# Attention, layer norm and MLP on one core: the first half of a hand-written instruction order replaced, with six more products of zeros

## The chip, the core and the metric

The kernel runs on one core of one Trainium2 chip, as one launch. The metric is the device time of that launch in microseconds (us). TensorE (PE) does matrix products and transposes into PSUM banks, VectorE (DVE) and ScalarE (ACT) read PSUM and write SBUF, GpSimd (POOL) works on SBUF alone, and SyncE (SP) issues DMA transfers. Each engine takes its instructions in the order of its own list and waits on semaphores for what the others produce. GpSimd issues transfers too, on another DMA queue (q0) than SyncE's (q1).

## The reference

Eight batches of eight heads, sequence 576, head width 64. Attention is causal, with a gate from a running sum; layer norm over the 512 joined columns follows, then an MLP of 512 to 2048 to 512 with a residual.

```python
s_pos = np.maximum(s, 0.0)
cum = np.cumsum(s_pos, axis=-1)
bias = -(cum[:, :, :, None] - cum[:, :, None, :])
scores = np.where(causal, -1000000000.0, scale * q @ k.T + np.minimum(bias, 0.0))
attn = np.exp(scores - scores.max(-1, keepdims=True))
attn = attn / (attn.sum(-1, keepdims=True) + 1e-09)
x = (attn @ v).transpose(0, 2, 1, 3).reshape(B, S, H * D)

xn = (x - mu) / np.sqrt(var + 1e-06) * g_ln
out = x + np.maximum(xn @ w_ch1, 0.0) @ w_ch2      # w_ch1 [512, 2048], w_ch2 [2048, 512]
```

## The kernel before

The whole kernel stands under a manual schedule: each engine's list is in the order in which the program issues the instructions, and that order is written by hand as a string of 1,238 words, `PLAN` (L1288). A loop behind it (L1371) splits every word into a step's name and its arguments and calls the step. A suffix (`:A`, `:D`, `:P`) names the engine that does it. A prefix `n*` sets `ahead[0] = n`: the next PSUM tile that is opened (`ptile`, L91) first gets n products of zeros (L101), which the step's own products overwrite. They have the width of the tile, 512 columns at most.

Batch 0 is done by rows of 128 (tiles 0 to 3, and a last one of 64 rows, 4), in two groups of four heads. For tile t and group g:

- `T.t.g` transposes the k and q rows (L958), `e.t.g` copies them out of PSUM (L156 on DVE, L154 on ACT);
- `S.t.g.i` is one bank of scores (L980, mask by L988), `x.t.g.i` its exponential on ACT (L997); `Sk` and `xk` are the last tile's remaining scores and their exponential (L1009, L1016);
- `V.t.g` weighs v (L1038), `N.t.g` divides by the sums on DVE (L1052, L1063);
- `L.t` is the layer norm (L724 on DVE), `X.t` its transposes (L757), `y.t` the copy out, `M`, `r` the first MLP product in pieces and its relu (L1082, L1093, L1095).

Batch 1 goes head by head: `Q`, `E` (transposes L336, copies L156 or L154), `s`, `d` (scores, L404, L412, L440, L448; their exponentials L415 come with them), `v` and `n` (L597, L609, L611), `ga` (statistics of the layer norm), `l` and `la` (L701, L724), `D` and `Da` (transposes of normed rows by DMA, L746).

Batches 2 to 7 go by pairs of heads. `lr` and `lv` load k, q and v rows on SyncE's queue (L219) into eight staging buffers; `cr` casts rows on GpSimd (L231); `tr` transposes by DMA on SyncE's queue (L238); `vm` and `vo` weigh v by the gate on GpSimd (L246, L258, L259); for batch 2 the transposes are on TensorE instead (`O2`, `F`, `G`, `lp`: L374, L154). `tk` copies the keys of the last tile (L158). `B2.n` is the burst of scores of pair n (L562), `bx` its exponentials on ACT (L567), `bm` the causal masks on GpSimd (L506), `Y.n.i` the weighing of v (L641), `K.n.i` the division on DVE (L658, L659, L661). `sd`, `se`, `sm` are the last tile's scores, exponential and mask of a batch.

Between these stand the units `u` and `U`, taken one by one from a queue that `qu`, `La` and `qm` fill. A unit is four products of 512 columns, either of the first MLP matrix (`ph`, L775), closed by a relu into `hT`, or of the second (`py`, L794), every fourth closed by the residual on DVE (`yo`, L806) and a store. With `u` the relu runs on ACT (L766), with `U` on DVE (L764).

`w2.i` loads a quarter of the second MLP matrix and `lp.n` the k and q rows of a pair of batch 2, both on GpSimd's queue. `aug` and `a3` write the gate's extra rows of the score operands by DMA on SyncE's queue (L278, L280); `a3` overwrites what `Sk` reads and so waits for it.

PSUM is shared out as m 2, s 3, t 2, o 1 banks for batches 0 and 1, and as m 2, s 6 after the word `to` (`to_pairs`, L1110). A tile waits until the last reader of the bank's former tile is done.

Of the kernel before, what the change touches and what calls it, by code (L numbers as in the profile page):

```python
# [30 lines left out]
def fast_path(  # L31
# [1256 lines left out]
    PLAN = """  # L1288
        relur.1 lr.3.0 relu.0 scan.0 scan.1 cq hi.0 qu.1 hi.1 sub.0 mid.0 lo.0 relur.2 sub.1 scan.2 W.4
        tc.0 bc.0 ck.0 6*T.0.1 T.0.0 mid.1 lo.1 tc.1 e.0.1:D bc.1 5*T.1.1 hi.2 sub.2 e.0.0:A S.0.0.0  # L1290
        T.1.0 W.1 m mid.2 lo.2 La.3 tc.2 e.1.1:D x.0.0.0 V.0.0 bc.2 e.1.0:A S.0.1.0 N.0.0 x.0.1.0
        S.1.1.0 x.1.1.0 T.2.1 bc.4 e.2.1:D S.1.1.1 x.1.1.1 T.2.0 S.1.0.1 x.1.0.1 e.2.0:D V.0.1 S.1.0.0
        N.0.1 S.2.1.2 x.2.1.2 T.3.0 x.1.0.0 e.3.0:D qu.2 S.2.0.2 S.2.1.0 x.2.0.2 aug L.0 x.2.1.0 T.3.1
        S.3.0.1 x.3.0.1 V.1.0 e.3.1:D qu.3 La.2 N.1.0 V.1.1 N.1.1 L.1 S.2.0.0 x.2.0.0 S.2.0.1 x.2.0.1
        S.3.0.2 x.3.0.2 X.0 y.0:A S.3.1.2 S.2.1.1 x.2.1.1 V.2.0 N.2.0 x.3.1.2 X.1 y.1:D S.3.0.0 x.3.0.0
        V.2.1 M.0.1.0 B.0.1 M.0.1.3 S.3.0.3 x.3.0.3 M.0.1.2 N.2.1 L.2 M.0.1.1 r.0.1:A M.0.0.0 M.0.0.2
        Q.q.4 B.1.1 O E.q.4.0:A M.0.0.3 E.q.4.1:A V.3.0 N.3.0 S.3.1.1 x.3.1.1 M.0.0.1 r.0.0:D S.3.1.3
        S.3.1.0 T.4.0 e.4.0:D X.2 y.2:D x.3.1.3 Q.k.4 E.k.4.0:D T.4.1 e.4.1:D x.3.1.0 S.4.0.1 x.4.0.1
        S.4.0.0 M.0.2.0 M.0.2.2 x.4.0.0 M.0.2.3 V.3.1 E.k.4.1:D N.3.1 B.2.1 S.4.1.1 x.4.1.1 u d.8 L.3
        M.0.2.1 Q.q.5 r.0.2:D B.1.0 s.8 u X.3 S.4.1.0 x.4.1.0 y.3:D Sk xk E.q.5.1:D E.q.5.0:A B.0.0  # L1300
        B.3.0 a3 u v.8 qu.4 qu.5 Q.k.5 lp.9 E.k.5.0:D u E.k.5.1:D V.4.0 N.4.0 s.9 cr.3.0.1 n.8 V.4.1
        N.4.1 Q.q.6 E.q.6.0:A u B.2.0 d.10 s.10 wr Q.k.6 E.k.6.0:D A.0 v.9 lp.10 w2.2 lr.3.1 E.k.6.1:D
        n.9 u U E.q.6.1:A s.11 Q.k.7 Q.q.7 E.q.7.0:A lp.11 La.6 E.k.7.0:D E.q.7.1:A U U E.k.7.1:D v.10
        n.10 cr.3.0.0 U d.12 s.12 U v.11 n.11 ga.1.0.0 A.2 d.14 s.13 O2.k.9:A u w2.3 B.3.1 v.12 n.12
        ga.1.0.3 s.14 O2.k.8:A A.1 me wT lv.2.0 wx vo.2:P U v.13 n.13 ga.1.1.2 s.15 cr.3.1.1 U O2.q.9:A
        ga.1.0.2 F.k.8 v.14 ga.1.0.1 F.k.9 G.k.9:A n.14 U u A.3 R vm.2.0:P lr.3.2 v.15 cr.3.2.0
        O2.k.11:A lv.2.1 lv.2.2 vm.2.1:P G.k.8:A ga.1.1.1 u lv.2.3 u O2.q.8:A ga.1.1.3 F.q.9 G.q.9:A
        n.15 ga.1.2.1 O2.q.11:A lv.2.4 lr.3.3 cr.3.2.1 cr.3.1.0 ga.1.2.0 ga.1.1.0 ga.1.2.3 ga.1.2.2 l.0
# [6 lines left out]
        bm.10.3 bx.10.1 Y.9.1 U K.9.1 u u tr.3.2.4 U u tr.3.4.5 bm.10.1 Y.10.1 lv.3.1 bm.10.0 B2.11
        bx.11.0 bx.11.4 lv.3.2 bx.11.5 lv.3.3 K.10.1 bm.10.2 Y.10.0 K.10.0 bm.11.2 ga.2.0.0 lv.3.4
        bx.11.2 bm.11.0 La.4 bx.11.1 u ga.2.1.2 ga.2.0.3 U u tk.3 cr.4.1.1 lr.4.2 bx.11.3 Y.11.0 K.11.0
        bm.11.3 u sd.3 U bm.11.1 u se.3 ga.2.0.1 lr.4.3 cr.4.0.1 vm.3.1:P Y.11.1 K.11.1 lv.4.0 lv.4.1
        vm.3.4:P lr.4.4 u ga.2.1.0 u B2.12 bx.12.0 vm.3.2:P U bx.12.4 bm.12.2 ga.2.1.1 bx.12.1 lv.4.2
        ga.2.2.0 cr.4.2.1 ga.2.2.1 ga.2.1.3 lv.4.3 la.2.0 la.2.1 cr.4.0.0 bx.12.5 bm.12.3 vm.3.3:P  # L1320
        cr.4.1.0 ga.2.2.2 bx.12.3 bm.12.1 u bx.12.2 bm.12.0 u u u B2.13 bx.13.5 bx.13.1 ga.2.0.2 la.2.2
        u bx.13.0 cr.4.4.0 sm.3 bx.13.4 tr.4.0.2 ga.2.2.3 u u bx.13.3 u Y.12.0 la.2.3 Da.2.0 bx.13.2
        bm.13.0 K.12.0 u u B2.14 cr.4.4.1 tr.4.4.5 bx.14.2 Y.12.1 K.12.1 lv.4.4 bx.14.1 bm.13.2 bx.14.3
        vo.4:P bx.14.4 u u u bx.14.5 bm.13.1 bx.14.0 Y.13.0 B2.15 bx.15.0 K.13.0 bx.15.2 lr.5.0 u
        cr.4.3.1 u vm.4.1:P bm.13.3 Y.13.1 bx.15.3 bx.15.5 bx.15.1 u K.13.1 cr.4.2.0 bx.15.4 bm.14.1
        cr.4.3.0 bm.14.2 bm.15.0 tr.4.2.4 tk.4 ga.3.0.0 U U bm.14.0 u bm.15.1 Y.14.0 K.14.0 bm.14.3
        Y.14.1 K.14.1 sd.4 ga.3.1.1 ga.3.1.3 ga.3.1.0 se.4 u vm.4.0:P u u bm.15.3 lv.5.0 Y.15.1 ga.3.0.1
        K.15.1 vm.4.3:P B2.16 bx.16.0 bx.16.2 vm.4.2:P bm.15.2 Y.15.0 K.15.0 sm.4 vm.4.4:P bx.16.3
        bx.16.1 bm.16.1 bx.16.5 bm.16.3 u ga.3.2.3 Da.1.4 bx.16.4 U bm.16.0 lr.5.1 cr.5.1.0 ga.3.1.2
# [5 lines left out]
        K.17.1 bx.18.4 cr.5.0.1 vm.5.2:P bx.18.5 bm.18.3 tr.5.2.4 u u ga.3.1.4 B2.19 vm.5.3:P bx.19.0
        bx.19.3 bm.18.2 vm.5.0:P bx.19.1 u ga.3.0.4 bm.18.0 bm.19.1 ga.4.0.1 bm.18.1 tr.5.0.2 u u lv.6.1
        sd.5 u u vm.5.1:P ga.3.2.4 la.3.4 bx.19.5 se.5 Y.18.1 sm.5 K.18.1 bx.19.2 U u u U ga.4.0.3
        bm.19.3 bx.19.4 bm.19.2 Y.18.0 u u ga.4.0.2 u K.18.0 ga.4.1.0 bm.19.0 Y.19.0 B2.20 bx.20.0
        vm.5.4:P ga.4.1.2 bx.20.2 lr.6.2 lr.6.3 cr.6.2.0 Y.19.1 K.19.1 K.19.0 ga.4.2.2 bx.20.3 bx.20.4
        bm.20.2 lv.6.2 bm.20.0 ga.4.2.3 u ga.4.2.0 u vm.6.1:P bx.20.5 bm.20.3 cr.6.0.1 bx.20.1 u u u  # L1340
        ga.4.1.1 bm.20.1 ga.4.0.0 Y.20.0 K.20.0 u u u u cr.6.3.1 lr.6.4 lr.7.0 cr.6.3.0 cr.6.4.0 lv.6.3
        Y.20.1 ga.4.2.1 vo.6:P B2.21 bx.21.4 bm.21.2 lr.7.1 la.4.0 la.4.1 u bx.21.1 cr.6.1.0 ga.4.1.3
        K.20.1 la.4.2 bx.21.2 bx.21.0 cr.6.4.1 bm.21.0 cr.6.2.1 u u bx.21.3 u u tr.6.4.5 Y.21.0 bx.21.5
        bm.21.3 B2.22 u bx.22.0 la.4.3 Da.4.0 bm.21.1 K.21.0 bx.22.4 cr.6.0.0 tr.6.0.2 bx.22.3 u u
        bx.22.5 bm.22.3 u Y.21.1 bx.22.2 La.7 K.21.1 cr.7.1.0 bx.22.1 bm.22.2 tk.6 u u vm.6.3:P tr.6.2.4
        B2.23 bx.23.2 bx.23.4 bx.23.0 bx.23.3 bm.22.0 bm.22.1 bx.23.1 u u u vm.6.0:P bx.23.5 bm.23.0 u
        sd.6 se.6 u u Y.22.1 u cr.7.0.1 K.22.1 ga.5.0.0 Y.22.0 K.22.0 ga.5.1.4 ga.5.0.1 u u bm.23.3
        lr.7.2 u vm.6.2:P cr.7.1.1 bm.23.1 Y.23.1 bm.23.2 B2.24 bx.24.0 Y.23.0 ga.5.0.3 K.23.0 lr.7.3
        lv.6.4 bx.24.3 K.23.1 ga.5.2.4 cr.7.3.0 lv.7.0 sm.6 ga.5.1.3 bx.24.4 bm.24.2 ga.5.2.0 u lv.7.1
# [255 lines left out]
```

## Time and profile before

Three runs took 347.36, 346.37 and 347.13 us: a median of 347.13 us. The profile is of one execution.

| what | value |
|---|---|
| time, median of 3 (lowest to highest) | 347.13 us (346.37 to 347.36) |
| the profiled execution's own time | 347.31 us |
| its span | 345.8 us |
| instructions | 8038 |
| mean granted TensorE clock | 0.996 of full speed |
| DMA | 48.61 MB, mean 141 GB/s over the span |
| one product of zeros (L101), its profiled length | 378 ns |
| first MLP products `ph` (L775) | 480, 109.8 us busy |
| second MLP products `py` (L794) | 583, 128.4 us busy |

The time of an execution is its span and some 1.5 us around it. Busy times are sums over instructions of one engine, where overlap counts once; a matmul's end is modelled, so that it counts as busy until its result would be there. The words that the change touches lie, in the trace, between 13.8 us (`S.1.1.1`) and about 175 us; to their left stand the first loads, the running sums and the first tile, to their right the rest of batches 3 to 7.

### The profile page before, as it was taken

The numbers are of one execution on the slowest core, as the hardware profiler recorded it, in microseconds if no ns is written. First come the engines' busy times: TensorE is split into PE (matmuls) and PEld (weight loads), VectorE is DVE, ScalarE is ACT, GpSimd is POOL, SyncE is SP. The second block draws the span as 40 slices with busy tenths as digits, with TensorE's granted clock in tenths as the row PEclk, the third lists the DMA queues.
The fourth block names the chain that finished last, engine by engine and source line by source line (L and its number), as shares of the span: only waits on it lengthen the run. The fifth ranks groups of instructions, "written<-read, shape, count | busy, mean of one in ns | idle before, by whom it ended". The sixth has DMA issues, their size and how long they took to land.

```text
span 345.8 us, 8038 instructions
## 1 busy us (share of the span) xinstructions
PE 333.7 (96%) x3079; PEld 185.5 (54%) x3105; DVE 205.1 (59%) x592; ACT 185.3 (54%) x343; POOL 168.2 (49%) x306
## 2 busy tenths in 40 slices
...
GB/s 151 180 192 175 199 194 199 205 249 214 193 224 249 156 246 179 162 252 218 164 197 176 229 101 138 138 2 2 121 63 0 30 124 46 2 78 44 2 63 66
DMA packets 147485, 48.61 MB, mean 141 GB/s; under 512 B 135184, under 2 KB 142896, under 8 KB 147440
## 3 DMA queue, kind: packets, MB, share of 16 engines
...
q14 instruction: 20, 0.16, 0.1%
...
## 4 chain that ended last, share of the span: by engine, by line
PE 82%; SPq 6%; DMA 4%; POOL 3%; DVE 2%; issue 1%; ACT 0%; DVEq 0%
PE ph L775 32%; PE py L794 32%; PE pot L641 7%; SPq L219 5%; DMA rowtmp<-in_v_dram 3%; PE sa L562 2%; PE sc L562 1%; PE sb L562 1%; POOL v_bf L246 1%; PE ph L1082 1%; PE st L980 1%; DMA hT<-in_s_dram 1%; POOL kq L231 1%; PE trt L958 1%; PE trt L101 1%
## 5 line engine op out<-in xcount | busy, mean ns | idle before, releaser
L794 PE MATMUL py<-w_bf,hT 128*128 128x512 bf16 (+2 forms) x583 | 128.4, 367 | 3.0 <-DVE yo L806 0.8
L775 PE MATMUL ph<-xT,w_bf 128*128 128x512 bf16 x480 | 109.8, 379 | 0.0
L766 ACT ACTIVATE hT<-ph 128x512 bf16<-128x512 f32 x97 | 58.0, 603 | 81.0 <-PE ph L775 79.7
L794 PEld LDWEIGHTS <-hT 128*128 128x128 bf16 x608 | 56.1, 98 | 62.6 <-issue 2.3
L775 PEld LDWEIGHTS <-w_bf 128*128 128x128 bf16 x544 | 51.0, 98 | 56.4
L506 POOL TENSOR_SCALAR_AFFINE_SELECT er<-er 128x256 bf16<-128x256 bf16 x96 | 38.6, 416 | 58.6 <-ACT er L567 43.5
L806 DVE SCALAR_TENSOR_TENSOR yo<-py,rstd,xb 128x512 f32<-128x512 f32 x32 | 24.0, 751 | 51.9 <-PE py L794 44.1
L764 DVE TENSOR_SCALAR hT<-ph 128x512 bf16<-128x512 f32 x39 | 26.8, 690 | 27.0 <-PE ph L775 26.2
L567 ACT ACTIVATE er<-sb 128x512 bf16<-128x512 f32 x48 | 28.1, 607 | 21.1 <-PE sb L562 14.3
L567 ACT ACTIVATE er<-sa 128x512 bf16<-128x512 f32 x48 | 28.6, 607 | 13.7 <-PE sa L562 12.4
L246 POOL TENSOR_TENSOR v_bf<-rowtmp,wt 128x512 bf16<-128x512 f32 (+1 forms) x30 | 32.4, 1085 | 1.9 <-DMA rowtmp<-in_v_dram 1.8
L641 PEld LDWEIGHTS <-er 128*128 128x128 bf16 x672 | 25.7, 97 | 9.7 <-issue 0.4
L567 ACT ACTIVATE er<-sc 128x512 bf16<-128x512 f32 x48 | 28.6, 611 | 4.1 <-PE sc L562 4.1
L641 PE MATMUL pot<-v_bf,er 128*128 128x66 bf16 x672 | 28.1, 193 | 0.1
L698 POOL TENSOR_TENSOR rstd<-rstd,mhalf 128x4 f32<-128x4 f32 (+1 forms) x8 | 8.8, 1098 | 37.4 <-DVE rstd L697 35.1
L231 POOL CAST kq<-rowtmp 128x512 bf16<-128x512 f32 (+1 forms) x30 | 20.0, 674 | 12.3 <-DMA rowtmp<-in_k_dram 12.2
L658 DVE TENSOR_REDUCE sums<-pot 128x5 f32<-128x10 f32 x48 | 8.0, 166 | 30.2 <-PE pot L641 29.8
L724 DVE SCALAR_TENSOR_TENSOR xn<-xb,mv,gb 128x512 bf16<-128x512 f32 x28 | 23.7, 846 | 1.0
L683 DVE BATCH_NORM_STATS2 stats<-xb 128x6 f32<-128x128 f32 (+1 forms) x84 | 23.8, 323 | 0.4
L661 DVE TENSOR_TENSOR xb<-pot,rinvs 128x256 f32<-128x256 f32 x48 | 20.4, 425 | 1.6
L562 PEld LDWEIGHTS <-kq 64*128 64x128 bf16 x360 | 11.2, 94 | 10.1 <-issue 4.7
L997 ACT ACTIVATE er<-st 128x512 bf16<-128x512 f32 x24 | 13.0, 605 | 3.0 <-PE st L988 2.5
...
## 6 DMA issues: line engine op xcount, KB each, us to landing
...
qp<-in_q_dram POOLq DMA_DIRECT2D x8, 144.0 KB, 10.1
...
```

Of the source, the lines that this page charges most:

```text
L246: e.tensor_tensor(out=v_bf[b % 2][0:pn, t, :, 0:D], in0=loaded.pop(("v", b, t))[0:pn], in1=wt[0:pn, t, b, :].unsqueeze(2).to_broadcast([pn ...
L506: nc.gpsimd.affine_select(out=out, in_=out, compare_op=ALU.is_ge, fill=0.0, base=0, pattern=pattern, channel_multiplier=-1,)
L562: nc.tensor.matmul(a, lhsT=lhsT, rhs=rhs, start=True, stop=True)
L567: nc.scalar.activation(out=er[:, 2 * n % 4 + i, o : o + 512], in_=bank["B", n].pop((name, i)), func=ACT.Exp, scale=scale,)
L641: nc.tensor.matmul(pot[:, t, :], lhsT=cols, rhs=v_bf[b % 2][:, kb, h, :], start=(kb == 0), stop=(kb == t),)
L683: nc.vector.bn_stats(out=st[b][:, t, part, :], in_=x_tiles(b)[t][:, lo:hi])
L724: nc.vector.scalar_tensor_tensor(out=xn, in0=tiles[t], scalar=mvs[b][:, t, 0:1] if b > 0 else mean0[:, t : t + 1], in1=gb, op0=ALU.subtrac ...
L764: nc.vector.tensor_scalar_max(out=dst, in0=ph, scalar1=0.0)
L766: nc.scalar.activation(out=dst, in_=ph, func=ACT.Relu)
L775: nc.tensor.matmul(ph, lhsT=w1_bf[:, kd, fb * P : (fb + 1) * P], rhs=xT[:, :, kd, :], start=(kd == 0), stop=(kd == KD - 1),)
L794: nc.tensor.matmul(py[t], lhsT=hT[:, fb, t * P : (t + 1) * P], rhs=w2_bf[:, fb, c0:c1], start=(fb == 0), stop=(fb == FB - 1),)
L806: nc.vector.scalar_tensor_tensor(out=yo, in0=py[t], scalar=rs, in1=x[:, c0:c1], op0=ALU.mult, op1=ALU.add)
```

## The change

Words 46 to 638 of `PLAN` are put in another order: from the second tile's scores (`S.1.1.0`) to the word before `qm`. The words before and behind are the same. The steps between are the same steps, with two exceptions:

- six `u` have become `U`: their relu is done on DVE instead of ACT;
- three words carry a prefix: `3*S.3.0.1`, `1*S.2.1.1` and `2*V.2.1`, six products of zeros more. They lie between the scores of batch 0's third tile (`S.2`) and those of its fourth (`S.3`).

The order of transfers changes with it. On SyncE's queue the rows of batches 2 and 3 came as lr.3.0, aug, a3, lr.3.1, lv.2.0, lr.3.2, lv.2.1 to lv.2.4, lr.3.3; now they come as lr.3.0, aug, a3, lv.2.0 to lv.2.3, lr.3.1, lv.2.4, lr.3.2, lr.3.3. Later, tr.3.0.2, tr.3.2.4, tr.3.4.5 are now tr.3.2.4, tr.3.0.2, tr.3.4.5, with lr.4.0 and lr.4.1 behind them and not ahead. On GpSimd's queue lp.9, lp.10, w2.2, lp.11, w2.3 becomes w2.2, lp.9, lp.11, w2.3, lp.10.

The beginning and the two ends of the diff:

```diff
-        T.1.0 W.1 m mid.2 lo.2 La.3 tc.2 e.1.1:D x.0.0.0 V.0.0 bc.2 e.1.0:A S.0.1.0 N.0.0 x.0.1.0
-        S.1.1.0 x.1.1.0 T.2.1 bc.4 e.2.1:D S.1.1.1 x.1.1.1 T.2.0 S.1.0.1 x.1.0.1 e.2.0:D V.0.1 S.1.0.0
-        N.0.1 S.2.1.2 x.2.1.2 T.3.0 x.1.0.0 e.3.0:D qu.2 S.2.0.2 S.2.1.0 x.2.0.2 aug L.0 x.2.1.0 T.3.1
-        S.3.0.1 x.3.0.1 V.1.0 e.3.1:D qu.3 La.2 N.1.0 V.1.1 N.1.1 L.1 S.2.0.0 x.2.0.0 S.2.0.1 x.2.0.1
-        S.3.0.2 x.3.0.2 X.0 y.0:A S.3.1.2 S.2.1.1 x.2.1.1 V.2.0 N.2.0 x.3.1.2 X.1 y.1:D S.3.0.0 x.3.0.0
-        V.2.1 M.0.1.0 B.0.1 M.0.1.3 S.3.0.3 x.3.0.3 M.0.1.2 N.2.1 L.2 M.0.1.1 r.0.1:A M.0.0.0 M.0.0.2
+        T.1.0 W.1 m mid.2 lo.2 La.3 tc.2 e.1.1:D x.0.0.0 V.0.0 bc.2 e.1.0:A S.0.1.0 N.0.0 x.0.1.0 qu.2
+        S.1.1.1 S.1.0.0 x.1.0.0 x.1.1.1 T.2.0 e.2.0:D S.1.0.1 x.1.0.1 T.2.1 e.2.1:D S.1.1.0 V.0.1 N.0.1
+        x.1.1.0 V.1.0 N.1.0 S.2.0.2 T.3.1 e.3.1:D S.2.1.2 x.2.1.2 S.2.1.0 x.2.1.0 V.1.1 N.1.1 T.3.0
+        e.3.0:D 3*S.3.0.1 x.3.0.1 L.1 S.2.0.0 x.2.0.0 x.2.0.2 L.0 1*S.2.1.1 S.2.0.1 x.2.0.1 bc.4 S.3.0.2
+        S.3.0.0 x.3.0.2 V.2.0 N.2.0 X.0 y.0:A S.3.1.2 x.3.0.0 X.1 y.1:D x.2.1.1 2*V.2.1 qu.3 qu.4
+        M.0.0.0 S.3.0.3 M.0.0.2 M.0.1.0 M.0.1.1 S.3.1.3 x.3.1.2 M.0.1.3 B.1.1 N.2.1 x.3.0.3 L.2 M.0.1.2
...
-        O2.k.10:A u u lr.3.4 vm.2.3:P vm.2.2:P cr.3.3.0 u F.q.8 G.q.8:A F.q.11 G.q.11:A u u O2.q.10:A
-        F.k.10 G.k.10:A F.k.11 G.k.11:A tk.2 qu.6 qu.7 F.q.10 G.q.10:A cr.3.3.1 vm.2.4:P to u lv.3.0
-        B2.8 bx.8.3 bx.8.0 vo.3:P bx.8.2 l.1 l.2 l.3 D u ga.1.0.4 u lr.4.0 lr.4.1 sd.2 se.2 sm.2
-        ga.1.1.4 bx.8.4 bm.8.2 bx.8.5 bx.8.1 bm.8.0 bm.8.3 bm.8.1 u cr.3.4.1 u tr.3.0.2 u B2.9 Y.8.0
+        G.q.11:A G.k.10:A ga.1.2.3 l.1 tk.2 l.2 l.3 cr.3.1.0 D lr.3.4 cr.3.2.0 vm.2.3:P cr.3.3.0 F.q.10
+        G.q.10:A cr.3.2.1 cr.3.3.1 to u B2.8 bx.8.0 bx.8.2 bx.8.4 bx.8.1 u bx.8.3 bm.8.1 sd.2 se.2 sm.2
+        u u u u bx.8.5 B2.9 bx.9.1 bx.9.3 bx.9.0 bx.9.5 bm.8.0 tr.3.2.4 lv.3.0 bm.8.2 Y.8.0 bm.8.3 Y.8.1
...
-        bm.17.1 tr.5.4.5 bx.17.5 bm.17.3 lr.6.1 u u qm u u cr.5.3.1 u lv.5.4 bm.17.0 cr.5.2.1 u tk.5
+        la.3.2 la.3.3 lr.6.1 lv.5.3 bx.17.0 qm u u cr.5.3.1 u lv.5.4 bm.17.0 cr.5.2.1 u tk.5 vo.5:P
```

More of the change, by code (lines that the diff above doesn't have):

```diff
@@ L1300, in fast_path @@
[L1300 to L1304, printed above, removed]
@@ L1315, in fast_path @@
[L1315 to L1319, printed above, removed]
@@ L1320, in fast_path @@
[L1320 to L1329, printed above, removed]
@@ L1335, in fast_path @@
[L1335 to L1344, printed above, removed]
@@ L1345, in fast_path @@
[L1345 to L1349, printed above, removed]
@@ new lines, in fast_path @@
+        S.3.0.0 x.3.0.2 V.2.0 N.2.0 X.0 y.0:A S.3.1.2 x.3.0.0 X.1 y.1:D x.2.1.1 2*V.2.1 qu.3 qu.4
+        M.0.0.0 S.3.0.3 M.0.0.2 M.0.1.0 M.0.1.1 S.3.1.3 x.3.1.2 M.0.1.3 B.1.1 N.2.1 x.3.0.3 L.2 M.0.1.2
+        Q.q.4 E.q.4.0:A qu.5 M.0.0.1 V.3.0 N.3.0 M.0.0.3 r.0.1:A S.3.1.0 x.3.1.0 E.q.4.1:A x.3.1.3
+        r.0.0:D T.4.0 e.4.0:D X.2 y.2:D S.3.1.1 T.4.1 e.4.1:D Q.k.4 S.4.0.0 x.3.1.1 x.4.0.0 M.0.2.0
+        M.0.2.3 M.0.2.2 B.0.0 E.k.4.0:D E.k.4.1:D B.0.1 S.4.0.1 V.3.1 S.4.1.1 x.4.1.1 U x.4.0.1 N.3.1
@@ new lines, in fast_path @@
+        B.3.1 B.2.0 aug s.8 d.8 u S.4.1.0 x.4.1.0 L.3 M.0.2.1 Q.q.5 r.0.2:D v.8 X.3 y.3:D u E.q.5.1:D
+        E.q.5.0:A u Q.k.5 E.k.5.0:D B.1.0 Sk xk Q.q.6 E.q.6.0:A E.q.6.1:A B.3.0 qu.6 a3 cr.3.0.0 w2.2
+        lp.9 B.2.1 E.k.5.1:D n.8 A.0 U U s.9 V.4.1 N.4.1 V.4.0 N.4.0 s.10 u d.10 Q.k.6 A.2 v.9 lp.11 A.1
+        E.k.6.0:D E.k.6.1:D w2.3 s.11 lv.2.0 u u n.9 d.12 s.12 wr La.6 v.10 lv.2.1 lv.2.2 lv.2.3 n.10 U
+        Q.q.7 E.q.7.0:A E.q.7.1:A O Q.k.7 E.k.7.0:D E.k.7.1:D U v.11 s.13 n.11 ga.1.0.3 ga.1.0.0
@@ new lines, in fast_path @@
+        O2.q.8:A lp.10 qu.7 wT d.14 wx O2.k.8:A vo.2:P U u v.12 n.12 s.14 U lr.3.1 lv.2.4 v.13 n.13
+        O2.k.9:A ga.1.0.4 F.k.8 ga.1.1.4 vm.2.1:P G.k.8:A U F.q.8 cr.3.0.1 ga.1.1.1 s.15 La.2 G.q.8:A
+        O2.q.9:A v.14 ga.1.1.3 ga.1.0.2 n.14 A.3 R u u vm.2.2:P me lr.3.2 vm.2.0:P lr.3.3 vm.2.4:P v.15
+        ga.1.1.2 n.15 ga.1.0.1 F.k.9 ga.1.1.0 ga.1.2.2 ga.1.2.1 u ga.1.2.0 F.q.9 O2.k.11:A O2.k.10:A
+        G.k.9:A G.q.9:A cr.3.1.1 l.0 u u u O2.q.11:A F.k.11 G.k.11:A F.q.11 u F.k.10 u O2.q.10:A
@@ new lines, in fast_path @@
+        G.q.11:A G.k.10:A ga.1.2.3 l.1 tk.2 l.2 l.3 cr.3.1.0 D lr.3.4 cr.3.2.0 vm.2.3:P cr.3.3.0 F.q.10
+        G.q.10:A cr.3.2.1 cr.3.3.1 to u B2.8 bx.8.0 bx.8.2 bx.8.4 bx.8.1 u bx.8.3 bm.8.1 sd.2 se.2 sm.2
+        u u u u bx.8.5 B2.9 bx.9.1 bx.9.3 bx.9.0 bx.9.5 bm.8.0 tr.3.2.4 lv.3.0 bm.8.2 Y.8.0 bm.8.3 Y.8.1
+        bm.9.3 K.8.0 bm.9.1 K.8.1 bx.9.4 bx.9.2 bm.9.2 tr.3.0.2 bm.9.0 vo.3:P cr.3.4.0 u u u Y.9.0 K.9.0
+        cr.3.4.1 tr.3.4.5 lv.3.1 lr.4.0 B2.10 bx.10.0 Y.9.1 lr.4.1 K.9.1 ga.2.0.2 ga.1.2.4 la.1.4
```

49 lines of the change are left out of this document (35 added, 14 removed).

## The prediction

> **What bounds the kernel now.** I read the page's totals first, then the busy time by stretch, then what TensorE waits for, then the chain of waits, then the DMA queues. Times are of the profiled execution: 347.31 us around a span of 345.8 us, 0.18 us above the median of 347.13 us. A difference under 0.3% (1.04 us) can't be told from none here.
>
> ```profile
> PE 333.7 (96%) x3079; PEld 185.5 (54%) x3105; DVE 205.1 (59%) x592; ACT 185.3 (54%) x343; POOL 168.2 (49%) x306
> ```
>
> TensorE is busy for 96% of the span, so the change can win only what lies in its gaps. By stretch (window, length, PE busy, then the weight loads and the other engines, clock, DMA):
>
> ```profile
> 13.80:20.00 6.20, 6.10 (x117) 5.91 (x115) 5.21 (x17) 5.49 (x11) 5.91 (x9) 1.00 1.63 196
> 20.00:30.00 10.00, 9.59 (x205) 9.20 (x206) 8.69 (x27) 8.26 (x16) 9.86 (x19) 1.00 1.48 188
> 30.00:41.00 11.00, 10.51 (x208) 9.53 (x205) 8.18 (x22) 8.73 (x17) 7.85 (x14) 1.00 1.62 187
> 41.00:60.00 19.00, 18.89 (x220) 11.62 (x220) 16.93 (x47) 17.38 (x34) 14.27 (x31) 1.00 1.25 196
> 60.00:65.00 5.00, 4.28 (x25) 2.00 (x24) 3.23 (x10) 3.11 (x5) 1.67 (x3) 1.00 0.99 200
> 65.00:70.00 5.00, 4.47 (x48) 2.64 (x49) 4.24 (x8) 3.68 (x6) 4.24 (x4) 1.00 1.16 218
> 70.00:75.00 5.00, 4.16 (x34) 1.91 (x27) 1.28 (x3) 2.98 (x6) 4.80 (x10) 1.00 1.05 228
> 80.00:175.00 95.00, 94.47 (x911) 50.57 (x918) 61.63 (x188) 59.38 (x112) 64.05 (x119) 1.00 1.01 202
> ```
>
> Length less PE busy gives 0.99 us idle from 13.8 to 41, 2.09 us in the 15 us from 60 to 75, and 0.53 us in the 95 us after 80. The granted clock is 1.00 throughout. A busy matmul includes its modelled drain (0.38 us for a product that is followed by the next after 0.216 us, as 16 ph products in 3.45 us show below), so each stall costs some 0.16 us more than its idle time. From the timeline's start times I therefore count losses as start to start, less the instructions' own spacing. The larger ones have names:
>
> ```profile
> PE py L794 <- DVE yo L806: 0.8, 1, 0.8
> PE py L794 <- DMA w_bf<-in_moe_w_ch_dram: 0.7, 1, 0.7
> PE trp L374 <- ACT kq L154: 0.5, 1, 0.5
> ```
>
> The chain that ended last runs on other engines in this stretch:
>
> ```profile
> 34.11 0.56 SPq L278
> ...
> 55.48 10.20 DMA rowtmp<-in_v_dram
> ...
> 65.76 1.04 POOL v_bf L246
> ...
> 77.48 0.63 PE pot L641 x15
> 78.10 3.45 PE ph L775 x16
> ```
>
> SyncE issues aug 3 at 34.11 (after Sk's scores), then the row loads of L219; a v row lands at 65.76; GpSimd weighs and casts back to back until its masks let Y.8.1 start at 77.48. After that the chain is TensorE. So two things set the end: TensorE's losses up to about 77 us, and GpSimd's masks there.
>
> The DMA queues between 37 and 64 us:
>
> ```profile
> q0 software_dynamic: 4289, 3.66, 83.5%
> q1 hardware_dynamic: 6126, 1.56, 36.1%
> ```
>
> Both move 5.22 MB in 27 us, some 193 KB/us, about what every 4 us slice shows between 13 and 64 us. Whoever starts later takes the same sum.
>
> **The change part by part.**
>
> *Zeros.* Six products: three in front of S.3.0.1, one at S.2.1.1 (128x512, 0.216 us apart), two at V.2.1 (128x260, half of that): 4 x 0.216 + 2 x 0.11 = 1.09 us. Three and two stand where TensorE waits anyway: S.3.0.1 for DVE's copy e.3.0 (0.69 us by L156's 68x1024 row), V.2.1 for the exponential x.2.1.1 (0.6 us by L997); hidden there, 0.87 us of them cost nothing. The one at S.2.1.1 runs after its buffer's wait and costs 0.22 us. I take the five as hidden; the bounds are 0.22 and 1.09 us. Zeros cannot buy clock: it is 1.00 already.
>
> *Head, 13.8 to 41 us.* The work is the same, in another order. I walked the new order by hand, each instruction starting at the latest of its engine's previous one and of what it needs, with these rows' durations (eight transposes 0.45, scores 0.28 to 0.34, exponentials each 0.48 after the last, copies 0.7 to 0.8, norms 0.62, layernorm 0.95, drain to reader 0.16 to 0.2). From 13.77 to the end of V.2.1, 7.44 us of work in both orders, before takes until 22.50 and so loses 1.3 us; the new order takes until 25.35, 11.58 us, 4.1 beyond its work: 1.09 of zeros, and waits around them (S.3.0.1 for e.3.0, S.2.1.1 for x.3.0.1's buffer, S.3.0.2 0.17, S.3.0.0 0.37, X.1 0.32, V.2.1 for x.2.1.1 0.76 with its zeros). From there to 41 us before loses 1.85 us (X.2 0.21, S.4.0.1 0.25, v.8 0.42, V.4.1 0.43, a unit 0.29, smaller ones), the new order 0.4 us at T.4.0 and little else.
>
> *Middle, 41 us to B2.8.* Before loses 0.31 (wT), 0.23 (v.15), 0.88 (the unit at 61.55, which waits for w2.3, landed 63.25), 0.64 (F.k.11 for ACT's copies) and 0.22 us: 2.28. After: POOL's queue now sends w2.2 ahead of lp.9, and lp.10 last, so w2.3 lands by about 60.5 and its reader comes at 63.7: that wait goes. lp.10, now the last of q0, lands at about 62.3 for O2.k.10 at 63.1. My walk leaves 0.13 (Q.k.6), 0.15 (v.14) and 0.45 us (v.15), and ACT runs continuously from 62.2 to 69.4, just ahead of F.q.11.
>
> *Sum to B2.8:* before 1.3 + 1.85 + 2.28 = 5.4 us beyond the work; after 4.1 + 0.4 + 0.7 = 5.2 us. Lead 0.2 us, B2.8 at 69.4 in place of 69.62.
>
> *B2.8 to Y.9.0.* The unit behind waits for VectorE's yo (L806, 0.75): 1.02 us before, 0.75 walked after, 0.27 won. Y.8.0 and Y.8.1 wait 0.5 us together for the masks before (done at 76.70 and 77.42). After, the masks are ready by about 75.0 and TensorE comes at 76.1 to 76.2, so 0.5 us is won. Lead 0.2 + 0.27 + 0.5 = 1.0 us; less 0.3 us for small stalls that such a walk misses (an estimate, about the unnamed part of the 1.85): 0.7 us.
>
> *Six relus to VectorE.* Each takes 0.69 us on DVE (L764) in place of 0.60 on ACT (L766): 4.1 us more on an engine at 59%, 3.6 us less on one at 54%. I walked them as parts of the lists; hidden by TensorE's own units (0.86 us per four products). Without that cover the next unit waits 0.09 us each, 0.5 us in all.
>
> *SP and the rows.* Sk's scores move from 33.4 to 38.7 us on TensorE; aug 3 waits for them (its rows are 34.11 to 36.53), and the whole stream of row loads behind it starts at 41.9 instead of 36.6, 5.3 us late. Queue order then puts v rows first (lv.2.0 to lv.2.3, lr.3.1, lv.2.4, lr.3.2, lr.3.3). q0 has its 193 KB/us to itself meanwhile and drains 1.2 us or more earlier (5.3 us x 45 KB/us that q1 had = 0.24 MB, over 193), and q1 then takes the whole rate, 210 to 250 KB/us after 63 us. So by 65 us the same bytes are in. I take nothing for it; the bounds are 0 and 5.3 us.
>
> *After 80 us.* TensorE has 0.53 us of idle time to give in 95 us, the list behind word 638 is the same, and what moves has slack: tr.3.4.5, tr.3.2.4, tr.3.0.2 and Da.2.0 keep ahead by my walk. I take nothing; bounds -0.3 and +2 us.
>
> Sum: 347.31 - 0.7 = 346.6 us on the profiled run, 346.4 us against the median. I take **346.5 us**.
>
> **The rivals.**
>
> *TensorE stalls less than I walked; GpSimd is the bound* (faster). The walk is worst at its 4.1 us to V.2.1, where before loses 1.3 on the same work. If half of that excess goes, Y.8.0 still waits for masks at 75.0: its start was 76.8, so the lead is at most about 1.7 us, plus 0.5 of Y.8.1's: 345.0 us, within 344.9 to 345.8. For it: GpSimd is 4.80 of 5.00 us busy from 70 to 75, so it gives nothing more.
>
> *The late row stream reaches the masks* (slower). Place: lr.3.3's landing, then GpSimd's casts cr.3.3.0, cr.3.2.1, cr.3.3.1 (0.61 each), then sm.2 and bm.8.0, bm.8.2, then Y.8.0. By my walk lr.3.3 lands at 70 to 71 for a cast at 71.5, and the masks have 0.8 us of slack; it decides from a landing at 72.3. If q1 does not catch up, masks end 77.42 + 5.3 = 82.7 and the time is 347.3 + 5.3 = 352.6 us; caught up except for 0.24 MB at 193 KB/us, the landing is 1.2 us later, and 1.2 to 2.6 us are lost: about 349 us. For it: between 37 and 60 us q1 got only 45 KB/us beside q0. Against it: the sum of the queues never falls.
>
> *Transposes too late in batches 2 and 3* (slower). tk.3 on GpSimd stands ahead of bm.10.0 and bm.10.3 and waits for tr.3.4.5, which lands at 87 to 88 by the 3.1 us of tr.3.2.4's issue row (83.91 to 87.05); Y.10.1 wants the masks at 90, slack 1 us. Ten units in a row precede it, so nothing else stands there for TensorE. The first MLP unit of batch 2 comes 3 us earlier than before (113.4 against 116.4) and wants Da.2.0, at about 112. Either missed by 2 to 3 us costs 1 to 2: 348.3 us.
>
> *The zeros are not hidden.* Then the five cost their 0.87 us: 347.4 us.
>
> *GpSimd against VectorE.* The weighing row L246 has median 1042 and longest 1475 ns in this kernel, the longest at 68.8 us, beside the xn of L724. In the new order three xn again run beside GpSimd's casts; three such delays of 0.43 us are 1.3 us, of which 0.8 is slack: 346.5 + 0.5 = 347.0 us. [...]
>
> **How the numbers follow.** Walk holds 0.36 (own range 345.4 to 348.2: 0.12 faster, 0.22 same, 0.02 slower); GpSimd the bound 0.20 (faster); late rows 0.19 (0.17 slower, 0.02 same); late transposes 0.15 (slower); zeros not hidden 0.05 (0.03 same, 0.02 slower); collisions 0.05 (same). Faster 0.32, same 0.32, slower 0.36. The range takes in GpSimd's bound at 344.9 and the slower cases to 349.6; beyond it lie the row stream that does not catch up and a walk that was wrong twice.
>
> **What would show it.** Right: TensorE's wait for w_bf at 63 us gone; V.2.1 (L1038) ending near 25.3 us, B2.8's first product (L562) at 69.3 to 69.5; Y.8.0 (L641) at 76.1 to 76.3 without a wait for masks; the stretch after 80 us as idle as before. Wrong: a first L641 product later than 76.8; GpSimd's casts (L231) waiting for rowtmp between 66 and 74 us; TensorE waiting for L506's masks at 88 to 92 us, or for xT at 112 to 117 us; idle time beyond 0.8 us in 80 to 175 us.

## The result and the profile after

The changed kernel takes 348.61 us in the median of 11 runs (348.19 to 349.41), the kernel before 347.49 us on the same chips (346.37 to 348.92): a ratio of 1.0034, 95% interval 1.0019 to 1.005, so 1.1 us slower. The forecast was 346.5 us. The profiled execution takes 348.68 us with a span of 347.1 us, 1.3 us above that of before.

The page's totals of the changed kernel, then the shares of the chain that ended last by engine, of the kernel before and of the changed one:

```profile
PE 336.7 (97%) x3111; PEld 186.4 (54%) x3111; DVE 210.7 (61%) x598; ACT 181.9 (52%) x337; POOL 170.9 (49%) x306
PE 82%; SPq 6%; DMA 4%; POOL 3%; DVE 2%; issue 1%; ACT 0%; DVEq 0%
PE 85%; DVE 7%; DMA 4%; issue 2%; ACT 1%; POOL 0%; DVEq 0%; ACTq 0%
```

VectorE has taken the place of SyncE and GpSimd in that chain. Busy time by stretch, same columns as before:

```profile
13.80:20.00 6.20, 5.96 (x106) 5.44 (x104) 4.98 (x18) 3.85 (x7) 5.91 (x8) 1.00 1.71 202
20.00:30.00 10.00, 8.46 (x154) 7.55 (x152) 6.00 (x20) 7.43 (x14) 9.86 (x19) 1.00 1.49 193
30.00:41.00 11.00, 11.00 (x231) 10.50 (x229) 9.43 (x23) 8.76 (x17) 7.74 (x13) 1.00 1.61 190
60.00:65.00 5.00, 5.00 (x62) 3.06 (x60) 4.05 (x17) 4.51 (x8) 3.93 (x7) 1.00 1.12 191
65.00:70.00 5.00, 4.54 (x39) 2.54 (x38) 4.83 (x10) 4.16 (x7) 3.60 (x5) 1.00 1.06 245
70.00:75.00 5.00, 4.39 (x40) 2.02 (x37) 2.17 (x4) 4.11 (x8) 4.88 (x7) 1.00 0.52 123
```

From 20 to 30 us TensorE is now idle for 1.54 us in place of 0.41. From 60 to 65 us the wait for w2.3 is gone, as forecast; from 65 to 75 us almost as much is idle as before (1.07 us against 1.37). Where it waits in the head, from the timeline of TensorE (start, length, line, and in brackets the idle time and its releaser):

```profile
18.68 0.81 PE L101 MATMUL st<-hT 128*128 128x512 bf16 x3
19.74 0.38 PE L980 MATMUL st<-kq 68*128 68x128 bf16 x4 [0.24 <-DVE kq L156]
...
20.93 0.38 PE L101 MATMUL st<-hT 128*128 128x512 bf16 x1 [0.46 <-ACT er L997]
...
24.35 0.39 PE L101 MATMUL pot<-hT 128*128 128x260 bf16 x2
...
25.26 0.42 PE L1038 MATMUL pot<-v_bf,er 128*128 128x65 bf16 x8 [0.40 <-ACT er L997]
```

Three zeros stand in the wait for e.3.0's copy, two in the wait for an exponential, and the one at S.2.1.1 comes behind its wait: each where the prediction had it. V.2.1 ends at 25.51 us (25.35 forecast, and this execution reaches V.0.0 at 13.32 us, 0.16 us later than that of before), against 22.50 us before. So TensorE is 3.0 us behind there. At B2.8 it is 1.44 us behind (71.06 against 69.62 us, forecast 69.4), at Y.16.1 0.98 us (133.70 against 132.72), and at B2.18 1.34 us (142.84 against 141.50), which is the whole difference of the spans.

A part that was not forecast is on VectorE. Its timeline, with GpSimd's of the time of the first xn behind it:

```profile
65.46 1.56 DVE L724 SCALAR_TENSOR_TENSOR xn<-xb,mv,gb 128x512 bf16<-128x512 f32 x1
67.05 1.41 DVE L806 SCALAR_TENSOR_TENSOR yo<-py,rstd,xb 128x512 f32<-128x512 f32 x2
...
137.53 1.98 DVE L724 SCALAR_TENSOR_TENSOR xn<-xb,mv,gb 128x512 bf16<-128x512 f32 x1
...
139.69 1.90 DVE L724 SCALAR_TENSOR_TENSOR xn<-xb,mv,gb 128x512 bf16<-128x512 f32 x1
141.50 1.40 DVE L806 SCALAR_TENSOR_TENSOR yo<-py,rstd,xb 128x512 f32<-128x512 f32 x2
```

```profile
65.44 2.48 POOL L246 TENSOR_TENSOR v_bf<-rowtmp,wt 128x512 bf16<-128x512 f32 x2
```

With no instruction of GpSimd's beside it an xn takes 0.75 us (at 68.83 us); these three, beside GpSimd's weighings, casts and masks, take 1.56, 1.98 and 1.90 us. The residual yo stands behind them on VectorE, and TensorE's next unit waits for yo:

```profile
67.86 1.02 PE L794 MATMUL py<-w_bf,hT 128*128 128x512 bf16 x4 [0.46 <-DVE yo L806]
```

The step at 67.86 us costs TensorE 0.62 us from start to start. Past 140 us it is another 0.36 us, but that one belongs to this execution: in a second profiled execution of the same kernel (run after_again) the xn at 65.61 us again takes 1.55 us and the same wait of 0.46 us follows, while the two later ones run almost undisturbed and TensorE loses nothing behind them:

```profile
137.67 0.75 DVE L724 SCALAR_TENSOR_TENSOR xn<-xb,mv,gb 128x512 bf16<-128x512 f32 x1
...
138.60 0.83 DVE L724 SCALAR_TENSOR_TENSOR xn<-xb,mv,gb 128x512 bf16<-128x512 f32 x1
```

Two theories came out of this: H, the head's 3 us are the loss, because the new order behind it has no waits left that would take them up; and P, VectorE's collisions with GpSimd are the loss. A third, Z, was that the six zeros cost their 1.09 us.

### The profile page after: what moved, and what is told of

The parts are those of the page before. It is cut to its first block, busy times and chain, and to the rows that moved or that the text cites. A ratio compares the mean times of both kernels' runs of the same rounds, so it can differ in the third digit from the quotient of the medians.

```text
span 347.1 us, 8075 instructions
## 1 busy us (share of the span) xinstructions
PE 336.7 (97%) x3111; PEld 186.4 (54%) x3111; DVE 210.7 (61%) x598; ACT 181.9 (52%) x337; POOL 170.9 (49%) x306
## 4 chain that ended last, share of the span: by engine, by line
PE 85%; DVE 7%; DMA 4%; issue 2%; ACT 1%; POOL 0%; DVEq 0%; ACTq 0%
PE py L794 33%; PE ph L775 32%; PE pot L641 6%; DMA w_bf<-in_moe_w_ch_dram 3%; PE sa L562 2%; PE sc L562 1%; PE sb L562 1%; DVE xn L724 1%; PE st L980 1%; DMA hT<-in_s_dram 1%; DVE stats L683 1%; PE pot L597 1%; PE trt L958 1%; PE ph L1082 1%; DVE yo L806 1%
## 5 line engine op out<-in xcount | busy, mean ns | idle before, releaser
L794 PE MATMUL py<-w_bf,hT 128*128 128x512 bf16 (+2 forms) x608 | 130.8, 368 | 1.1 <-DVE yo L806 1.1
L766 ACT ACTIVATE hT<-ph 128x512 bf16<-128x512 f32 x93 | 55.5, 604 | 80.0 <-PE ph L775 78.5
L764 DVE TENSOR_SCALAR hT<-ph 128x512 bf16<-128x512 f32 x43 | 29.4, 689 | 26.7 <-PE ph L775 26.0
L724 DVE SCALAR_TENSOR_TENSOR xn<-xb,mv,gb 128x512 bf16<-128x512 f32 x28 | 26.1, 932 | 1.0
L231 POOL CAST kq<-rowtmp 128x512 bf16<-128x512 f32 (+1 forms) x30 | 19.3, 658 | 10.0 <-DMA rowtmp<-in_k_dram 9.9
```

The lines of the kernel that those rows point to most:

```text
L724: nc.vector.scalar_tensor_tensor(out=xn, in0=tiles[t], scalar=mvs[b][:, t, 0:1] if b > 0 else mean0[:, t : t + 1], in1=gb, op0=ALU.subtrac ...
L764: nc.vector.tensor_scalar_max(out=dst, in0=ph, scalar1=0.0)
L766: nc.scalar.activation(out=dst, in_=ph, func=ACT.Relu)
L794: nc.tensor.matmul(py[t], lhsT=hT[:, fb, t * P : (t + 1) * P], rhs=w2_bf[:, fb, c0:c1], start=(fb == 0), stop=(fb == FB - 1),)
```

## The experiments

All are other orders of the same steps; two change the number of zeros, two the engine of relus, and nothing is left out of the computation. Ratios are to the kernel before on the same chip.

**The new order without its zeros.**

```diff
-3*S.3.0.1 ... 1*S.2.1.1 ... 2*V.2.1
+S.3.0.1 ... S.2.1.1 ... V.2.1
```

> The new order without its six products of zeros. If the zeros are what the change costs (theory Z), they go with their whole 1.09 us: about 347.5 us, no more than the kernel before. If they lie in waits (theory H, the new order's head waits for copies and exponentials whatever TensorE does meanwhile), only the one at S.2.1.1 is won, 0.2 us: about 348.4 us, and V.2.1 ends 25.1 to 25.4 us into the span.

Measured: 349.13 us, ratio 1.0049 (1.0019 to 1.0078), but the runs differ in the granted clock. Six took 348.65 to 349.28 us at a mean clock of 0.996 to 0.997, about the changed kernel's time; four took 350.56 to 352.47 us at 0.983 to 0.987. The profiled execution (350.56 us) is one of the four. Its stretches:

```profile
19.00:20.00 1.00, 0.30 (x6) 0.31 (x7) 0.96 (x5) 0.00 (x0) 1.00 (x2) 1.00 1.98 173
...
22.00:23.00 1.00, 0.81 (x10) 0.68 (x9) 0.00 (x0) 1.00 (x2) 1.00 (x3) 0.59 2.05 182
...
28.00:29.00 1.00, 1.00 (x12) 1.00 (x11) 0.30 (x1) 0.17 (x1) 1.00 (x2) 0.50 1.24 202
29.00:30.00 1.00, 1.00 (x22) 1.00 (x20) 0.00 (x0) 0.00 (x0) 1.00 (x3) 1.00 1.77 177
```

TensorE waits 0.90 us for e.3.0 with nothing to do, until 19.70 us. Some 2.5 us later its clock is granted at half, from 22.2 to 29.0 us (0.59 is the mean of a stretch that begins at full clock), though the longest gap on the way there is the 0.90 us. Both executions do the first tile at the same time within 0.05 us. TensorE is 0.24 us ahead of the changed kernel at S.2.1.1, where the one zero outside a wait is gone, but at the next scores, S.2.0.1, only 0.04 us (21.39 against 21.43): they wait for an exponential that ends at 21.34 us (21.37 in the changed kernel). By 29.1 us, where the full clock is back, it is 2.1 us behind. Theory Z falls: the six zeros cost no time that lasts. In these runs they keep the clock up: without them it falls in four of ten runs, with them in none of the changed kernel's 23 does the mean come near those four (0.994 at the least). From 19 to 22 us, just ahead of the fall, TensorE was busy for 1.75 of 3 us (0.30, 0.54 and 0.91). What sets it off, and why in some runs only, was not shown.

**The old order with the same six zeros.**

```diff
-S.3.0.1 ... S.2.1.1 ... V.2.1
+3*S.3.0.1 ... 1*S.2.1.1 ... 2*V.2.1
```

> The old order with the six products of zeros in front of the same steps (three at S.3.0.1, one at S.2.1.1, two at V.2.1). There TensorE has no wait of that size, so V.2.1 ends about 1 us later than in the kernel before (23.3 to 23.6 us). Theory Z: that lateness stays, +1.1 us, 348.6 us. Theory A (lateness of the head is absorbed by the waits that end at a fixed time, for w2.3 at 63.3 us and for the masks at 77.4 us): between 0 and +0.3 us, 347.5 to 347.8 us.

Measured: 347.76 us, ratio 1.0005 (0.9988 to 1.0022). V.2.1 comes 1.0 us later than before, reckoned from V.0.0; B2.8 0.4 us later, B2.18 0.2 us later. Theory A holds: the old order takes up most of a microsecond of lateness in its waits behind, among them the one for w2.3, which is gone from this trace.

**The new order up to V.2.1, the old one behind it.** The plan is the new words up to 2*V.2.1 and qu.3, then aug, La.2 and x.3.1.2, then the old words from M.0.1.0 on.

```diff
-V.2.1 M.0.1.0 B.0.1 M.0.1.3 S.3.0.3
+2*V.2.1 qu.3 aug La.2 x.3.1.2 M.0.1.0 B.0.1 M.0.1.3 S.3.0.3
```

> The new order up to V.2.1 (with its zeros), the old order behind it. Theory H: V.2.1 ends 3.0 us later than before, as in the new order; the old order's waits for w2.3 (0.9 us) and for the masks (0.5 us) take up 1.4 us, the rest stays: +1.6 us, about 349.1 us. Theory P (VectorE held up by GpSimd behind the head is the whole cost): the old rest has none of the new collisions, so no more than the zeros' 0.2 us is lost: 347.7 us.

Measured: 348.62 us, ratio 1.0029 (1.0015 to 1.0044). Of the head's 3.0 us some 1.1 remain in the time, less than the 1.6 expected, but some five times what P allows. (In the profiled execution, reckoned from V.0.0, it is 2.85 us at V.2.1 and 1.5 us past 140 us.) The head alone is enough for a loss as large as the change's.

**The new order with two layer norms behind the residuals.**

```diff
-cr.3.1.1 l.0 u u u O2.q.11:A
+cr.3.1.1 u u u l.0 O2.q.11:A
...
-la.3.2 la.3.3 lr.6.1 lv.5.3 bx.17.0 qm u u cr.5.3.1
+la.3.2 lr.6.1 lv.5.3 bx.17.0 qm u u la.3.3 cr.5.3.1
```

> The new order with two layer norms of VectorE moved behind the residuals that had to wait for them: l.0 behind the next two units' yo, la.3.3 behind the unit after qm. Theory P (VectorE's xn takes 1.56, 1.98 and 1.90 us beside GpSimd instead of 0.75, and the residual behind it comes late): TensorE's waits for yo at 67.9 us (0.46 us) and at 141.1 to 142.3 us (0.36 us) go, -0.8 us, about 347.8 us. Theory H: what is won there is lost again at the next wait, no more than 0.2 us is won: 348.4 us.

Measured: 347.93 us, ratio 1.0011 (0.9997 to 1.0025), some 0.6 to 0.7 us under the changed kernel by the medians. The intervals of the two ratios overlap, so the trace has to decide. TensorE runs as in the changed kernel, 0.16 us later throughout, up to the unit at 67.86 us, and wins 0.63 us there: the first step as P has it. The second step (0.36 us at 142.30 us) is there too against the profile of the changed kernel shown above, but as after_again does not lose that time either, it can't be put down to the move of la.3.3. Of TensorE's waits for a residual, the one behind B2.8 is left:

```profile
PE py L794 <- DVE yo L806: 0.6, 1, 0.6
```

So both H and P carry part of the loss, P with the one xn that stands ahead of a residual at 65 us. That the collision makes it late, and not its place alone, is read from the lengths: it takes 0.81 us more than an undisturbed xn, and TensorE loses 0.62 us.

**The old order up to V.2.1, the new one behind it, and the same with the two layer norms moved.**

```diff
-2*V.2.1 qu.3 qu.4 M.0.0.0 S.3.0.3 M.0.0.2
+V.2.1 qu.4 M.0.0.0 S.3.0.3 M.0.0.2
```

> The old order up to V.2.1, the new order behind it (no new zeros). Theory H: the head's 3.0 us at V.2.1 are the loss, and the new middle and later parts regain 1.6 us of it on their own; together with the old head they run ahead of the kernel before as far as TensorE sets the pace: B2.8 at 68 to 69 us and about 346.0 us, 1.5 us under the kernel before and 2.6 under the changed one. Theory P (the collisions of VectorE with GpSimd behind the head are the whole loss): they are still there, so about the changed kernel's 348.4 us. In between, 347.5 us: what the head wins is taken by waits with a fixed end.

> The same with l.0 and la.3.3 moved behind the residuals as in the run a_xn. If head (H) and collisions (P) add up: 0.7 us under h_headbefore, about 345.3 us by H. If with the other timing of the head the collisions do not meet, the same as h_headbefore.

Measured: 347.29 us, ratio 1.0007 (0.998 to 1.0033), and 346.91 us, ratio 0.9987 (0.9965 to 1.0009). Neither H's 346.0 us nor P's 348.4 us came, and the second kernel is not at 345.3 us. The third outcome that was named, 347.5 us because waits with a fixed end take what the head wins, is the one that did. From the timeline of TensorE in the first:

```profile
35.18 0.28 PE L597 MATMUL pot<-v_bf,er 128*128 128x65 bf16 x4 [0.88 <-DMA v_bf<-in_v_dram]
36.39 0.63 PE L597 MATMUL pot<-v_bf,er 128*128 128x65 bf16 x6 [0.93 <-DMA v_bf<-in_v_dram]
```

The new order goes to v.8 soon after Q.q.5. Coming 3 us earlier, it waits 2.1 us (2.3 in the second) for batch 1's v rows, which land no earlier for it: the last of these waits ends at 36.39 us (36.97 in the second), and the changed kernel starts v.8 at 36.19 us without one. The second kernel is 2.5 us ahead of the changed one at v.8 and 0.2 us behind it after v.8. Here too the clock then falls in some runs: in the first kernel four runs of twelve took 349.1 to 349.9 us at 0.993 to 0.995, and its profiled one has

```profile
35.00:41.00 6.00, 4.89 (x71) 4.70 (x71) 1.64 (x3) 1.74 (x3) 4.67 (x9) 0.72 1.29 201
```

The late head hid this wait in the changed kernel.

**Old order to word 179, new one behind, with the layer norms moved; and the same without the move.** The old part now holds v.8, Sk and aug 3, and reaches v.8 at 34.7 us.

```diff
-... a3 u v.8 qu.4 qu.5 Q.k.5 lp.9 E.k.5.0:D u E.k.5.1:D V.4.0 N.4.0 s.9 ...
+... a3 u v.8 qu.4 qu.5 Q.k.5 lp.9 E.k.5.0:D u B.3.1 B.2.0 Q.q.6 E.q.6.0:A E.q.6.1:A qu.6 cr.3.0.0 w2.2 ...
```

> The old order up to word 179 (k of batch 1's pair 5, about 36 us), with Sk and aug 3 at their old places, the new order behind it, with l.0 and la.3.3 moved as in a_xn. The runs h_headbefore and h_hb_xn let TensorE wait 2.1 to 2.3 us for batch 1's v rows at 34 to 37 us; the old order reaches them at 34.8 us without that wait. If that wait was what kept the old head's 3 us from being won (theory V), this runs ahead of the kernel before: the new middle's 0.6 us, the waits for w2.3, yo and the masks: 345.5 to 346.3 us, 1.2 us or more under the kernel before. If the early row stream (aug 3 at 34 us, the v rows first) brings its own waits, or if something else holds the new middle: about h_hb_xn, 0.3 us under the kernel before.

> As h_cut41, but with l.0 and la.3.3 where the new order has them. If head and collisions add up, the collisions cost here what they cost in the new order, 0.5 to 0.8 us above h_cut41: 347.1 to 347.4 us, 0.4 us under the kernel before. If with the earlier clockwork l.0 does not meet GpSimd's weighing, or the residual has slack there: within 0.2 us of h_cut41, 346.4 to 346.8 us.

Measured: 346.62 us, ratio 0.9967 (0.9947 to 0.9987), and 346.66 us, ratio 0.9965 (0.9947 to 0.9984). Both are faster than both kernels, 1.1 us under the kernel before, just short of the 1.2 us that theory V asked for. TensorE reaches B2.8 at 67.49 and 68.26 us, and Y.8.0 at 75.10 and 75.38. Without the move, l.0 again takes 1.56 us (at 62.66) and TensorE waits 0.4 us for a residual; with it, TensorE waits about as long for one of ScalarE's copies (L154). What the second is later than the first, 0.8 us at B2.8 and all of it there already behind a wait for v rows at 35 us, shrinks to 0.3 us where both come to GpSimd. The waits of the first there:

```profile
PE pot L641 <- POOL er L506: 0.6, 1, 0.6
PE sd L533 <- POOL kz L158: 0.6, 1, 0.6
```

So GpSimd's masks at about 75 us are the next bound, as the rival on the faster side had it. Behind word 179 the order of the second kernel is the new one, less the steps that the old part has done already: TensorE is 2.3 us ahead of the changed kernel at 39.5 us, 2.8 us at B2.8 and 2.4 us at 132 us. Nothing of the lead over the changed kernel is given back there.

**Every unit's relu on its old engine.** The k-th unit takes the engine of the old order's k-th unit: 20 of 293 words change, 13 from `U` to `u` and 7 the other way, six relus in the balance.

```diff
-S.4.1.1 x.4.1.1 U x.4.0.1 ... A.0 U U s.9 ... s.11 lv.2.0 u u n.9
+S.4.1.1 x.4.1.1 u x.4.0.1 ... A.0 u u s.9 ... s.11 lv.2.0 U U n.9
```

> The new order with every unit's relu on the engine that it has in the old order at the same place of the count (the six relus back on ACT). Theory U (the six relus on VectorE hold up residuals and copies there): 0.5 us won, 348.1 us. Theories H and P: no change beyond 0.2 us, 348.4 to 348.8 us.

**One relu alone back on ScalarE.**

```diff
-S.4.1.1 x.4.1.1 U x.4.0.1
+S.4.1.1 x.4.1.1 u x.4.0.1
```

> The new order with one relu more on ScalarE: that of the first unit (word 148), ahead of s.8's exponentials. In the run a_units, where 13 relus went to ScalarE and 7 to VectorE, TensorE fell 0.8 us behind at s.8 (34.1 us). If that came from this one relu in front of ScalarE's exponentials: TensorE falls 0.5 to 0.8 us behind at the same place and about 0.6 us stay, 349.1 us. If it came from the sum of the swaps: no more than 0.2 us, 348.5 to 348.7 us.

Measured: 351.1 us, ratio 1.0096 (1.0061 to 1.0131), and 349.2 us, ratio 1.004 (1.0023 to 1.0056). Theory U falls: the change of engines is no loss as a whole, and at s.8 the relu on VectorE wins. In the second kernel, TensorE's timeline shows the price of the one relu at s.8:

```profile
34.99 0.30 PE L404 MATMUL sc<-kq 68*128 68x320 bf16 x1 [0.62 <-ACT er L997]
```

In the changed kernel the same product starts at 34.11 us without a wait. The relu stands ahead of an exponential on ScalarE, and s.8 waits for that one: 0.88 us there, of which 0.73 to 0.76 are still there from 37 to beyond 100 us; reckoned from V.0.0, which this execution reaches 0.10 us later, 0.63 to 0.66. The times alone (intervals 1.0023 to 1.0056 and 1.0015 to 1.0044) would not tell this kernel from the changed one. In the first kernel the same place costs 0.8 us and v.10 (49.4 us) another 1.1: it waits for VectorE (L618), whose list there holds two relus that the new order has on ScalarE. So the engine of a relu is worth something place by place, and in both directions.

**The old order up to B2.8's first exponentials, the new one behind.**

```diff
-B2.8 bx.8.3 bx.8.0 vo.3:P bx.8.2 l.1 l.2 l.3 D u ga.1.0.4 u lr.4.0 lr.4.1 sd.2 ...
+B2.8 bx.8.3 bx.8.0 vo.3:P bx.8.2 l.1 l.2 l.3 D ga.1.0.4 ga.1.1.4 bx.8.4 bx.8.1 u bm.8.1 sd.2 ...
```

> The old order up to the first exponentials of batch 2's first pair (B2.8), the new order behind it. As the prediction had it, the new part wins there: yo's wait 0.27 us and the masks' waits 0.5 us go, less 0.36 us at the residual behind la.3.3: -0.4 us, about 347.1 us. If the part behind B2.8 is what makes the change slower: above 348 us.

Measured: 348.26 us, ratio 1.0013 (0.9986 to 1.004): unclear, and no win. Its profiled execution is 0.1 us behind the kernel before at B2.8, 0.6 at B2.9 and 0.3 at B2.18: the tails wait 1.3 us for GpSimd's copy (L158), a wait that neither the kernel before nor the changed one has. This suggests that the new part behind B2.8 needs the new middle's order on GpSimd; no run shows it.

**The changed kernel again.**

> The changed kernel as it is, beside the run before it on the same chip: 1.1 us above the kernel before as measured, 348.4 to 348.7 us; this says how far the hybrids' differences hold on one chip.

Measured: 348.5 us, ratio 1.0029 (1.0015 to 1.0044), on the chip of h_cut41. The expectation holds.

**The new order with one copy earlier.**

```diff
-V.1.1 N.1.1 T.3.0 e.3.0:D 3*S.3.0.1
+T.3.0 e.3.0:D V.1.1 N.1.1 3*S.3.0.1
```

> The new order with T.3.0 and its copy e.3.0 two words earlier, ahead of V.1.1 and N.1.1; all else as it is, zeros too. Theory H (the new head's loss is one chain: VectorE does N.1.1 before e.3.0, S.3.0.1 waits for that copy, and ScalarE's exponentials come after it): the copy ends some 0.8 us earlier, V.2.1 follows by 0.6 to 0.8 us, and that much stays at the end: 347.8 us. If the loss before 25 us is taken up later anyway, or if ScalarE's list is what sets V.2.1: no more than 0.2 us, 348.4 us.

Measured: 347.99 us, ratio 1.0013 (0.9998 to 1.0027), 0.5 to 0.6 us under the changed kernel by the medians, with intervals that overlap. The copy now starts at 18.56 in place of 19.0 us: T.3.0 sets it, so 0.44 us are won and not 0.8, and reckoned from V.0.0, which this execution reaches 0.09 us earlier, 0.35 us.

```profile
19.30 0.38 PE L980 MATMUL st<-kq 68*128 68x128 bf16 x4
```

This lead is there at every step from S.3.0.1 (19.30 for 19.74) to 132 us, without loss or gain. Theory H holds step by step: what is late here in the new order stays late.

## Why the prediction was wrong

- **Zeros.** Place right, and five are hidden as forecast. The sixth was priced at 0.22 us; it costs 0.2 us at S.2.1.1 and nothing from S.2.0.1 on, which waits for ScalarE either way. "Zeros cannot buy clock: it is 1.00 already" was wrong. It was read from the old order's clock; in the new order without the zeros it fell to 0.50 in the profiled run (a_nozero), and four of ten runs lost 1.8 us and more.
- **Head.** V.2.1 right: 25.35 us forecast, 25.51 measured, 0.16 us of it from before V.0.0.
- **Middle, the step that failed.** The sum to B2.8 let the new order regain 3.05 us between V.2.1 and B2.8; it regained 1.57. From V.2.1 to 41 us the changed kernel loses 0.7 us and not 0.4 (T.4.0 0.35, T.4.1 and v.8 0.12 each). From 41 us it loses 1.7 us and not 0.7. Of the three losses walked there, v.14 and v.15 did not come and Q.k.6 cost 0.32 in place of 0.13; what came is 0.62 at the unit behind F.q.11, where yo is late behind the long xn; 0.32 at Q.k.6, which starts at 45.56 us just behind the norm N.4.0 (L1061, to 45.42; the waits of a_xn name it), and that stands on VectorE behind two of the relus that the new order does there (L1095 and L764, 43.05 to 44.3); 0.31 at wT, whose five products take 0.45 us in either order and were counted as a loss of before alone; the rest in small gaps. w2.3's wait is gone as forecast. (The old order's 0.64 us, put at F.k.11, is F.q.10's, at 68.41 us; the price stands.)
- **B2.8 to Y.9.0.** Right: the wait for yo is 0.77 us (0.75 forecast), and Y.8.0 waits for no mask, though at 78.00 us it comes later than the 76.8 us that was to show the forecast wrong. From B2.8 to Y.16.1 TensorE regains 0.46 of its 1.44 us, about the 0.47 us of the sum (0.27 + 0.5 - 0.3). But the masks' wait, put down as 0.5 us won, was only what a kernel that comes later does not meet.
- **Six relus.** The bounds, 0 and 0.5 us of loss, excluded a gain. One relu alone is worth 0.6 us (a_unit1). The row of ACT at 54% was an average; at s.8 ScalarE's exponentials are the bound. Elsewhere two relus on VectorE stand ahead of a wait of 0.3 us (Q.k.6, above); that these relus make it late was not tried.
- **SP and the rows.** Right: the row stream that starts 5.6 us later (42.18 for 36.57 us; 5.3 forecast) costs nothing that the trace shows; 65 to 70 us moves 245 GB/s.
- **After 80 us.** Taken as nothing, and idle time did not grow: 0.20 us in place of 0.53. The 0.36 us that one profiled execution lost at the residual behind la.3.2 and la.3.3 (141 us) did not come again in the other one.
- **Rivals.** The slower rivals that had most weight (late rows, late transposes) did not happen. "GpSimd against VectorE" did, with the other engine as the one that holds TensorE up: it was costed from GpSimd's weighing (1.475 us) and its slack, while three of VectorE's xn took 0.8 to 1.2 us longer and TensorE lost 0.62 and 0.36 us behind yo. The old order's trace had this to show: 1.475 us is the longest weighing up to 180 us only (1.551 at 199.3 us), and VectorE's xn had taken longer there too, in the line below and at 198.5 us (1.48 us). Either engine's instruction can be the longer one, or both: in the changed kernel xn takes 1.56 us beside two weighings that together take 2.48 in place of 2.08 us.

```profile
66.15 1.20 DVE L724 SCALAR_TENSOR_TENSOR xn<-xb,mv,gb 128x512 bf16<-128x512 f32 x1
```

In sum, by runs: the new order up to word 179 costs about 2 us (1.8 by the medians of after_again and h_cut41_raw, 2.2 by their ratios), the new order behind it wins about 1.1 us (346.66 against 347.76). Inside the first figure a_e30 shows 0.35 us as one wait; the collision at 65 us is worth about 0.6 us where TensorE sets the pace (a_xn) and next to nothing where GpSimd's masks do (h_cut41 against h_cut41_raw). How much each further wait of the head costs was not tried.
